# The last expert of a weight load split unevenly over the transfer engines, in an attention and mixture-of-experts kernel

## The chip, the core and the metric

The kernel runs on one core of a Trainium2 chip. A core has a matrix engine (PE, and PEld for its weight loads), a vector engine (DVE), a scalar engine (ACT), GpSimd (POOL), SyncE (SP) and sixteen transfer engines that move data between the chip's memory and the core's on-chip memory of 128 partitions. The metric is the device time of one execution in microseconds (us); lower is better.

## The reference

Attention over 8 batches, 8 heads, 576 positions and 64 numbers a head, with a mask that is a plain window of 32 positions for the first four heads and a dilated one (every fourth of the last 128) for the others. The result, 4608 rows of 512, goes through a soft mixture of 8 experts with 4 slots each:

```python
logits = x @ phi
d = softmax over the rows of logits
slot_input = d.T @ x                      # 32 slots, 4 an expert
for e in range(E):
    h = np.maximum(slot_input[e] @ w1[e], 0.0)   # w1[e]: 512 x 1024
    slot_out[e] = h @ w2[e]                      # w2[e]: 1024 x 512
c = softmax over the slots of logits
out = c @ slot_out
```

All inputs and the output are 32-bit floats in the chip's memory. The kernel works in 16 bits; the loads convert on their way.

## The kernel before

The work is staged as a software pipeline over the eight batches, with an order of steps written out by hand (ORDER). Each batch loads q, k and v (`load_raw`, L201), turns them (L231), forms scores, exponentials and masks, multiplies by v, and from the attention rows forms logits and the running sums of the slot inputs. All transfers of weights, inputs and outputs are issued from POOL's queue, and one list of transfers is worked off in the order of issue, each transfer spread over the sixteen engines.

Weights are loaded between the batches' inputs. The list EARLY holds w1 of experts 0 to 4 one by one, w1 of experts 5 to 7 together, and w2 of experts 0 to 2 together; `load_weights` takes the next ones from it, and `load_full` (L207 for w1, L212 for w2) issues each as one transfer of 128 rows an expert:

```python
EARLY = [(1, e, e + 1) for e in range(5)] + [(1, 5, 8), (2, 0, 3)]
```

One row of w2 of an expert is 4096 numbers, 16 KB in memory and 8 KB on the core. When the input tiles come free, a second transfer loads w2 of experts 3 to 5 (`load_full(late, 2, 3, 6)`, L212 too), and `load_half` (L220) loads w2 of experts 6 and 7 by halves of the columns: expert 6 whole in its half, expert 7 in two quarters, first the left half, then the right.

After the attention stage, PE multiplies the slot inputs by w1 (L608), turns the hidden values (L618), and `emit_so` (L641) accumulates the products with w2, experts 0 to 3, then 4, 5, and the left halves of 6 and 7. `gather_so` (L652) and `spread_so` (L657, L658) bring the left half of the slots' outputs into place, `emit_fin` (L664, L673, L677) forms output tiles of 128 rows, and `emit_batch` issues their stores (L686) from POOL. The right halves of experts 6 and 7 are worked in among the first six batches; the remaining rows are stored last (L713).

Of the kernel before, what the change touches and what calls it, by code (L numbers as in the profile page):

```python
# [10 lines left out]
FP16 = mybir.dt.float16  # L11
# [16 lines left out]
N_SLOTS = 32  # L28
# [16 lines left out]
    (("P", 3), ("P", 4), ("L", 0), ("L", 1), ("D", 0)),  # L45
    (("D", 1), ("D", 2), ("D", 3)),
)
ORDER = """
MD0.2 MK2.2 AP4.2 ET.3 VBc.1 S1.1 MK0.1 RP4.2 ED.3 E1.1 AD1.2 EP.3 VC.1 RD1.2 MP4.2
VCc.1 ER.3 MD1.2 AD3.2 VA.1 QT0.0 AP3.2 RD3.2 VAc.1 QT1.0 RP3.2 MD3.2 S2.1 KT1.0  # L50
# [3 lines left out]
"""  # L54
STEPS = [(w.split(".")[0], int(w.split(".")[1])) for w in ORDER.split()]
ON_ACT = ('D3', 'P0', 'P1', 'P3')
# [40 lines left out]
def kernel(  # L97
# [10 lines left out]
    nc = tc.nc  # L108
# [5 lines left out]
    consts = ctx.enter_context(tc.tile_pool(name="consts", bufs=1))  # L114
# [3 lines left out]
    ident = cst[:, o : o + 128]  # L118
    spread = cst[:, o + 128 : o + 256]
    quad = cst[:, o + 256 : o + 260]  # L120
    masks = consts.tile([128, NMASK], FP16, name="masks")
    phi_raw = consts.tile([128, 4, N_SLOTS], FP16, name="phi_raw")
    phi4 = consts.tile([128, 4, 4, N_SLOTS], FP16, name="phi4")
# [14 lines left out]
    def weights_tile(pool, which, e0, e1):  # L138
        n = (4 * FDIM, 8 * DMODEL)[which - 1]
        t = pool.tile([128, e1 - e0, n], FP16, name=f"w{which}_{e0}", tag=f"w{which}_{e0}")  # L140
        for e in range(e0, e1):
            of = t[:, e - e0]
            if which == 1:
                w1t[e] = of.rearrange("p (c f) -> p c f", c=4)
            else:
                w2t[e] = of.rearrange("p (c n) -> p c n", c=8)
        return t

    EARLY = [(1, e, e + 1) for e in range(5)] + [(1, 5, 8), (2, 0, 3)]
    early_tiles = {x: weights_tile((w1_pool, w2a_pool)[x[0] - 1], *x) for x in EARLY}  # L150
# [54 lines left out]
    def load_full(t, which, e0, e1):  # L205
        if which == 1:
            nc.gpsimd.dma_start(  # L207
                out=t.rearrange("p e (u x) -> p (e u) x", u=2),
                in_=moe_w1[e0:e1].rearrange("e (u p c) f -> p (e u) (c f)", u=2, p=128),
            )  # L210
        else:
            nc.gpsimd.dma_start(  # L212
                out=t, in_=moe_w2[e0:e1].rearrange("e (p c) n -> p e (c n)", p=128)
            )

    def load_half(e, s, n):
        src = moe_w2[e].rearrange("(p c) n -> p c n", p=128)
        cols = slice(DH * s, DH * s + DH)
        for u in range(0, 8, n):
            nc.gpsimd.dma_start(out=w2t[e][:, u : u + n, cols], in_=src[:, u : u + n, cols])  # L220
# [249 lines left out]
    for which in "QK":  # L470
        load_raw(which, 1)
    nc.gpsimd.dma_start(
        out=phi_raw.rearrange("p (u c) s -> p u (c s)", u=2),
        in_=moe_phi.rearrange("(u p c) s -> p u (c s)", u=2, c=2),
# [8 lines left out]
    def load_weights(n):  # L483
        for _ in range(n):
            x = weights.pop(0)
            load_full(early_tiles[x], *x)

    tmp = {}

# [37 lines left out]
    def loads(which, b):  # L527
        load_raw(which, b)
        if which == "V":
            if b > 2:  # L530
                load_weights(1)
            if b == B - 1:
                load_weights(len(weights))
# [6 lines left out]
    for it in range(B + max(s for _, s in STEPS)):  # L540
        for op, stage in STEPS:
            b = it - stage
            if not 0 <= b < B:
                continue
            step(op, b)
            if op in frees and b + 2 < B:
                loads(frees[op], b + 2)
            left.discard((op, b))
            if w2b_pool is None and not left:
                raw_pool.release()  # L550
                w2b_pool = tc.alloc_tile_pool(name="w2b", bufs=1, side="right")
                late = weights_tile(w2b_pool, 2, 3, 6)
                slab_weights(6, "qk0", QK_SLAB)
                slab_weights(7, "qk1", QK_SLAB)
                load_full(late, 2, 3, 6)
                for s in range(2):
                    for e in (6, 7):
                        load_half(e, s, 8 if e == 6 else 4)
        if it == 0:
            nc.vector.tensor_copy(  # L560
                out=phi4, in_=phi_raw[:, :, None, :].broadcast_to([128, 4, 4, N_SLOTS])
            )
# [40 lines left out]
    for fc in range(2):  # L603
        for g in range(2):
            for dc in range(4):
                for j in range(4):
                    e = 4 * g + j
# [9 lines left out]
    for c in range(8):  # L617
# [3 lines left out]
        out=hTm[:, 0].rearrange("p c (j s) -> p c j s", j=4)[:, :, :, 0:16], in_=hT4[:, :, :, 0:16]  # L621
    )
    nc.scalar.copy(
        out=hTm[:, 1].rearrange("p c (j s) -> p c j s", j=4)[:, :, :, 16:32], in_=hT4[:, :, :, 16:32]
# [87 lines left out]
    for e in range(2):  # L712
        nc.gpsimd.dma_start(  # L713
            out=rest[:, e, 512:576, :].rearrange("n i d -> i n d"), in_=om_l[64 * e : 64 * e + 64]
# [37 lines left out]
```

## Time and profile before

| what | before |
|---|---|
| median of 3 runs (lowest to highest) | 178.29 us (178.06 to 178.37) |
| the profiled execution, its own time | 178.29 us |
| its span, first to last instruction | 176.5 us |
| busy: PE, DVE, ACT, POOL | 123.5, 126.0, 123.5, 38.4 us |
| moved by the transfer engines | 40.83 MB counted on the core's side, 231 GB/s |
| read from and written to memory | 62.07 MB and 9.44 MB, 405 GB/s over the span |
| second three-expert load (L212) issued | 105.57 us |
| first output store (L686) issued | 149.40 us |
| last output store (L713) issued | 166.97 us |

Busy times are shares of a span in which stages differ: until some 125 us the batches' pipeline runs on PE, DVE and ACT, then the experts' weights are awaited and used, and from 149 us outputs are stored. The row of the transfer engines counts packets; loads that convert from 32 to 16 bits show half of what they read. The chain of waits is followed back from the last instruction, so it shows which wait set the end and not which engine was busiest.

### The profile page before, as it was taken

The numbers are of one execution on the slowest core, as the hardware profiler recorded it, in microseconds if no ns is written. First come the engines' busy times: TensorE is split into PE (matmuls) and PEld (weight loads), VectorE is DVE, ScalarE is ACT, GpSimd is POOL, SyncE is SP. The second block draws the span as 40 slices with busy tenths as digits, with TensorE's granted clock in tenths as the row PEclk, the third lists the DMA queues.
The fourth block names the chain that finished last, engine by engine and source line by source line (L and its number), as shares of the span: only waits on it lengthen the run. The fifth ranks groups of instructions, "written<-read, shape, count | busy, mean of one in ns | idle before, by whom it ended". The sixth has DMA issues, their size and how long they took to land.

```text
span 176.5 us, 4724 instructions
## 1 busy us (share of the span) xinstructions
PE 123.5 (70%) x2004; PEld 80.9 (46%) x2004; DVE 126.0 (71%) x275; ACT 123.5 (70%) x266; POOL 38.4 (22%) x60
## 2 busy tenths in 40 slices
PE   0026928998888888988989888978677295778300
PEld 0015616676566566656766557656332142221000
DVE  6473899999999999999999998465130104878500
ACT  6007758999999999999999999995501104888300
POOL 7321022112112112116000002710000001856600
PEclk9999999969999999999789999996858969655555
DMA  5999999999999999999999999999999999999997
GB/s 83 215 214 210 214 212 215 215 213 214 216 212 217 211 218 215 208 215 220 213 211 217 213 218 216 222 210 225 213 213 221 192 198 175 340 398 397 401 415 209
DMA packets 18981, 40.83 MB, mean 231 GB/s; under 512 B 1169, under 2 KB 11537, under 8 KB 18193
## 3 DMA queue, kind: packets, MB, share of 16 engines
q0 software_dynamic: 18816, 40.41, 113.8%
q8 instruction: 15, 0.25, 0.5%
q1 hardware_dynamic: 144, 0.14, 0.3%
q14 instruction: 6, 0.04, 0.1%
HBM read 62.07 MB, written 9.44 MB: 405 GB/s over the span
## 4 chain that ended last, share of the span: by engine, by line
ACT 38%; DMA 27%; DVE 14%; PE 10%; issue 2%; POOL 2%; POOLq 0%; ACTq 0%
DMA w<-in_moe_w_dram 19%; ACT p L282 10%; DMA phi_raw<-in_moe_phi_dram 8%; ACT vX L253 7%; ACT xp L337 7%; DVE qk L231 5%; PE f L664 5%; ACT om L673 3%; ACT xT L376 3%; ACT xT L378 3%; DVE p L293 3%; DVE vT L231 3%; ACT xd L337 2%; PE s L273 2%; PE rp L357 2%
## 5 line engine op out<-in xcount | busy, mean ns | idle before, releaser
L282 ACT ACTIVATE p<-s 128x1920 f16<-128x1920 f32 (+1 forms) x24 | 44.6, 1857 | 10.2 <-PE s L273 10.1
L273 PE MATMUL s<-qk 32*128 32x128 f16 (+2 forms) x704 | 26.7, 295 | 18.4 <-DVE qk L231 12.0
L253 ACT COPY vX<-rv 128x768 f16<-128x768 f16 (+1 forms) x32 | 27.8, 943 | 1.8 <-PE rv L247 1.8
L316 PEld LDWEIGHTS <-p 128*128 128x128 f16 (+1 forms) x480 | 22.4, 103 | 13.3 <-DVE xp L341 4.0
L337 ACT ACTIVATE xp<-o_P,rc_P 128x64 f16<-128x64 f32 x96 | 26.5, 497 | 2.2 <-DVE rc_P L328 2.2
L273 PEld LDWEIGHTS <-qk 32*128 32x128 f16 x704 | 17.3, 117 | 21.6 <-DVE qk L231 12.0
L293 DVE TENSOR_TENSOR p<-p,masks 128x1920 f16<-128x1920 f16 (+1 forms) x24 | 25.7, 1084 | 0.2
L231 DVE STREAM_TRANSPOSE qk<-rawQ 128x576 uint32<-128x576 uint32 x16 | 18.8, 1243 | 2.7 <-DMA rawQ<-in_q_dram 2.7
L316 PE MATMUL o_P<-vX,p 128*128 128x65 f16 (+1 forms) x288 | 20.0, 205 | 0.8 <-ACT xp L337 0.2
L231 DVE STREAM_TRANSPOSE qk<-rawK 128x576 uint32<-128x576 uint32 x16 | 19.5, 1231 | 0.4 <-DMA rawK<-in_k_dram 0.4
L247 PE MATMUL rv<-cst,vT 128*128 128x128 f16 x176 | 17.5, 242 | 3.2 <-DVE vT L231 1.8
L231 DVE STREAM_TRANSPOSE vT<-rawV 128x576 uint32<-128x576 uint32 x16 | 19.4, 1223 | 0.5 <-DMA rawV<-in_v_dram 0.5
L686 POOL DMA_DIRECT2D out_dram<-om x15 | 11.1, 744 | 39.2 <-DVE om L677 34.8
L247 PEld LDWEIGHTS <-vT 128*128 128x128 f16 x176 | 13.2, 124 | 7.5 <-issue 3.7
L677 DVE TENSOR_SCALAR om<-f,rrow 128x256 f16<-128x256 f32 (+1 forms) x28 | 13.5, 519 | 3.5 <-PE f L664 2.9
L664 PE MATMUL f<-so_sb,ET 32*128 32x256 f16 (+1 forms) x60 | 12.5, 392 | 3.9 <-ACT om L673 2.7
L673 ACT ACTIVATE om<-f,rrow 128x256 f16<-128x256 f32 (+1 forms) x28 | 12.8, 503 | 2.6 <-PE f L664 2.0
L376 ACT COPY xT<-rp 128x576 f16<-128x576 f16 x16 | 11.5, 909 | 1.3 <-PE rp L357 1.3
L316 PE MATMUL o_D<-vX,p 128*128 128x65 f16 x128 | 9.9, 202 | 2.5 <-DVE xp L341 2.0
L201 POOL DMA_DIRECT2D rawQ<-in_q_dram x8 | 5.1, 633 | 29.4 <-DVE rc_P L328 18.4
L378 ACT COPY xT<-rd 128x576 f16<-128x576 f16 x16 | 10.6, 795 | 0.0
L341 DVE TENSOR_TENSOR xd<-o_D,rc_D 128x256 f16<-128x256 f32 x24 | 9.9, 412 | 0.2
(81 smaller groups left out, 176.7 us busy)
## 6 DMA issues: line engine op xcount, KB each, us to landing
w<-in_moe_w_dram POOLq DMA_DIRECT2D x3, 3072.0 KB, 35.5
out_dram<-om POOLq DMA_DIRECT2D x11, 512.0 KB, 4.6
w<-in_moe_w_dram POOLq DMA_DIRECT2D x5, 1024.0 KB, 15.9
rawQ<-in_q_dram POOLq DMA_DIRECT2D x8, 576.0 KB, 12.7
rawK<-in_k_dram POOLq DMA_DIRECT2D x8, 576.0 KB, 11.4
rawV<-in_v_dram POOLq DMA_DIRECT2D x8, 576.0 KB, 11.6
out_dram<-om POOLq DMA_DIRECT2D x2, 1024.0 KB, 7.3
w<-in_moe_w_dram POOLq DMA_DIRECT2D x2, 512.0 KB, 36.7
```

Source lines behind the costliest of these rows:

```text
L231: nc.vector.transpose(out=out_, in_=in_)
L247: nc.tensor.transpose(rg[:, n_t, :, c, :], rows, ident)
L253: copy(out=vX[b % 2][:, t0 : t0 + n, :, 0:D], in_=rg.rearrange("p n h c d -> p n h (c d)"))
L273: nc.tensor.matmul(sps[:, h, c0 : c0 + w], kk, qq, start=(tt == 0), stop=(tt == 1))
L282: return nc.scalar.activation(out=pt, in_=sps[:, :, 0:n], func=AF.Exp, scale=SCALE)
L293: return nc.vector.tensor_tensor(out=pt, in0=pt, in1=m, op=ALU.mult)
L316: nc.tensor.matmul(o[rows, h, :], lhs, rhs, start=(n == 0), stop=(n == len(jobs) - 1), skip_group_check=True,)
L337: nc.scalar.activation(out=dst[:, h], in_=src[:, h], func=AF.Copy, scale=rc[:, h : h + 1])
L376: copy(out=xT_t[b][:, c, :], in_=rg[:, 0:S])
L378: copy(out=xT_t[b][:, 2 + c, :].rearrange("p (i r) -> p i r", r=DIL), in_=rg[:, :, 0:SUB].rearrange("p r i -> p i r"),)
L664: nc.tensor.matmul(fp[:, 0 : c1 - c0], ET[32 * j : 32 * j + 32, m : m + 128], so_sb[32 * j : 32 * j + 32, c0:c1], start=True, stop=True,)
L673: nc.scalar.activation(out=dst, in_=fp[:, 0 : c1 - c0], func=AF.Copy, scale=rrow[:, blk : blk + 1])
```

## The change

Expert 2 of the early w2 load becomes transfers of its own: 112 rows, then 8, then 8, with three tiny transfers of 13, 8 and 11 rows of 32 numbers (rows of phi, written to a tile that nothing reads) between and behind them. Experts 0 and 1 go as one transfer of the same form as before. The program has six more transfers, all on POOL's queue; every other engine's instructions are the same and in the same order. A transfer whose rows are a multiple of 16 gives each engine the same number of rows. The code takes it that one of fewer rows than 16 uses as many engines as it has rows, starting where the one before it ended, so that 13, 8, 8, 8 and 11 rows, 48 in all, bring that place back to where it was.

```diff
+CURSOR = 13
...
+    aside = consts.tile([16, 3, N_SLOTS], FP16, name="aside")
...
+    def step_cursor(i, n):
+        nc.gpsimd.dma_start(out=aside[0:n, i], in_=moe_phi[0:n])
+
+    def load_uneven(t, e):
+        src = moe_w2[e].rearrange("(p c) n -> p (c n)", p=128)
+        nc.gpsimd.dma_start(out=t[0:112], in_=src[0:112])
+        step_cursor(0, CURSOR)
+        nc.gpsimd.dma_start(out=t[112:120], in_=src[112:120])
+        step_cursor(1, 8)
+        nc.gpsimd.dma_start(out=t[120:128], in_=src[120:128])
+        step_cursor(2, (-CURSOR - 24) % 16)
...
     def load_weights(n):
         for _ in range(n):
             x = weights.pop(0)
-            load_full(early_tiles[x], *x)
+            which, e0, e1 = x
+            if which == 1:
+                load_full(early_tiles[x], 1, e0, e1)
+            else:
+                load_full(early_tiles[x][:, 0 : e1 - e0 - 1], 2, e0, e1 - 1)
+                load_uneven(early_tiles[x][:, e1 - e0 - 1], e1 - 1)
```

## The prediction

> **What bounds the kernel now.** I read the page first: the rows of the DMA and of its queues.
>
> ```profile
> DMA  5999999999999999999999999999999999999997
> GB/s 83 215 214 210 214 212 215 215 213 214 216 212 217 211 218 215 208 215 220 213 211 217 213 218 216 222 210 225 213 213 221 192 198 175 340 398 397 401 415 209
> ...
> q0 software_dynamic: 18816, 40.41, 113.8%
> q8 instruction: 15, 0.25, 0.5%
> ...
> q14 instruction: 6, 0.04, 0.1%
> ```
>
> The sixteen transfer engines are busy from the second slice to the last, so work for them is what the time is made of, and every engine drains its own share in order of issue. The one thing that they don't share evenly is the code: 15 packets of queue q8 bring 0.25 MB, that is 16 KB each, and a packet is one engine's alone. The chain of waits shows where unevenness counts (start, us, what), and the waits name the same pair (us in total, times, longest):
>
> ```profile
> 111.58 0.74 POOL w L220
> 112.33 34.05 DMA w<-in_moe_w_dram
> 146.37 0.04 issue
> 146.41 0.32 PE so L641 x4
> 146.73 0.02 issue
> 146.76 0.43 DVE so_part L652
> ...
> PE so L641 <- DMA w<-in_moe_w_dram: 3.0, 2, 2.3
> ```
>
> At 146.37 the second quarter of expert 7 is complete. It is complete when the slowest of sixteen engines has delivered, and PE, the gather, the spread and the first output store follow at once. Behind it the transfers never run dry: the landings of the output stores follow each other by 1.31 to 1.34 us per 512 KB up to 175.23, about 23.5 us of stores that no engine can shorten. So a shift of the 146.37 us landing shifts the end one for one.
>
> The landing records hold sixteen times for each transfer, one an engine. For the transfer of 146.37 they are: seven engines at 143.71 to 144.47, three at 144.84 to 144.87, six at 145.96 to 146.37. For the first load they all lie within 0.4 us. I sorted the packets into sixteen chains (a packet starts 19 ns before the end of the one ahead of it, so the chains separate). A 16 KB code packet takes 0.89 to 1.07 us and leaves its engine about 1.1 us later for good. Eight engines take the fifteen packets in turn, starting again with the ninth at 86.07. By 146.37 six have been hit twice (the six last ones), two once. The 8 KB packets of q14 add 0.32 us each to three of the other eight. This is the unevenness that the change can touch: give the eight hit engines fewer rows.
>
> **The change part by part.** Before, one transfer brought w2 of experts 0 to 2, 8 rows an engine for each expert. After, experts 0 and 1 go as before; expert 2 goes as 112 rows (7 an engine) and twice 8 rows. If the 13-row transfer leaves the next one to start at engine 13, the two pieces lie on 13, 14, 15, 0 to 4 (the 8-row step goes round to 13 again, the 11-row step back to 0): these eight carry 9 rows of expert 2, engines 5 to 12 carry 7.
>
> *One row.* The 24 rows of the later three-expert transfer take its slowest engine from 126.47 to 141.10: 14.63 / 24 = 0.61 us. So 0.61 us later on the eight heavy engines, 0.61 us sooner on the light ones, and all of it persists, since no engine idles until 149.
>
> *Six more transfers.* On an engine a transfer ends with a 4-byte packet. A 576 KB load repeats every 2.76 us, of which eight packets are 8 x 0.342 = 2.74: 0.02 us for the end. Six times: 0.13. The tiny rows: the phi load has 16 packets of 128 bytes an engine and lands 0.25 us behind the load ahead of it, at most 0.016 us a row; three rows: 0.04. Together 0.16 us on every engine, on the path. From below: 0.1 if the ends hide; from above: 0.3 at 0.05 a transfer.
>
> *Issue.* POOL gets six more issues at some 0.7 us, 4 us in all. They cost nothing, since POOL stands idle there:
>
> ```profile
> 81.33 0.81 POOL L212 DMA_DIRECT2D w<-in_moe_w_dram  x1
> 105.57 0.77 POOL L212 DMA_DIRECT2D w<-in_moe_w_dram  x1 [23.43 <-DVE rc_P L328]
> 106.34 0.90 POOL L220 DMA_DIRECT2D w<-in_moe_w_dram  x1
> ```
>
> The built program has eight completion semaphores in rotation, and an issue waits for the landing of the eighth transfer before it. With six more, the last tiny transfer waits for the fifth w1 load (97.11), the second three-expert load for the 3 MB w1 load (111.91, so it is issued at 112 and not at 105.57), and the six of expert 6 and 7 for landings at 121 to 127. Queued behind them on POOL is only the next load. Engines reach the second three-expert load at 124 to 126 and expert 6 at 138 to 141, so 10 us of cover are left. [...] The first store waits for the last tiny transfer (about 127), not later than now.
>
> *Which engines.* No record names an engine. Records that start in the same nanosecond stand in the file in an order that is no accident: about thirty such pairs whose two chains I can tell apart fit, without one contradiction, a file sorted by engine number as text, with the hit engines being 1 to 8 and hit in the order 4, 5, 6, 7, 8, 1, 2, 3. That is an inference, and it matters more than any price above. If the numbers of the change are the same numbers, light engines 5 to 12 hold only half of the hit ones. Engines 5 to 8 come 0.61 sooner, but 4 and 1, both hit twice by 146.37, get a row more. They stand 2.25 and 2.34 us behind the foremost now (145.96 and 146.05 against 143.71), the last one (engine 6, which started 0.4 us late) 2.66. The new last is 2.34 + 0.61 = 2.95, or 0.29 later than now.
>
> *The sum.* +0.29 (engine 1 is last) + 0.16 (six transfers) = +0.45 us. The profiled execution took 178.29 us (span 176.5, 1.8 around it), which is also the median of the runs shown: 178.74.
>
> *A cost no row shows.* A heavy piece puts 8 rows on 8 neighbouring partitions at once. The nearest row is the store of 64 partitions, sixteen engines on half of the rows: it moves 512 KB in 1.25 us, as the 128-partition store does (2.5 us for 1 MB), so half of the rows cost nothing, and I take 0. From above, a row that takes twice its time costs 0.61 a piece, 1.2 for two, and only where engines arrive together: engines 1 to 3 do. That widens the range upwards; half of it, 0.6, is in the range.
>
> [...]
>
> **The rivals.** *Aligned: faster.* The count that the change turns may stand elsewhere than at 0 when the program starts, or number engines differently, so that the light eight are exactly the hit eight. Then the six late ones land 0.61 sooner (146.37 to 145.76), the others at most 144.87 + 0.61 = 145.48, so the gate moves by -0.61 + 0.16 = -0.45 us: 177.84. For it: the spread is two groups of eight and the change shifts eight against eight by one row, the right size. Against it: my numbering. It decides as soon as no twice-hit engine is heavy.
>
> *No turning: slower.* An 8-row transfer may always begin with engine 0. Both pieces then lie on 0 to 7, five of the six twice-hit engines get a row more, engine 6 among them: +0.61 + 0.16 = +0.77, 179.06. The change would not do what it says. The trace of before has no transfer under 64 rows and can't speak to it. [...]
>
> *Another offset.* The heavy eight lie anywhere else: at least one twice-hit engine is heavy for all but one offset in sixteen, so +0.2 to +0.77.
>
> **How the numbers follow.** Half overlap 0.36, aligned 0.30, no turning 0.20, another offset 0.14. A difference under 0.2% (0.36 us) can't be told from none. Of the half overlap (0.45 with some 0.15 either way) about 0.10 falls under it, of the aligned case (0.45) 0.02, of other offsets 0.02: same 0.14. Faster 0.28, slower 0.58. The range must hold the aligned case with its low overhead and the slow cases with part of the neighbouring-row cost: 177.7 to 179.4. The likeliest case's own range is 178.55 to 179.3.
>
> **What would show it.** The sixteen landings of the second quarter of expert 7: likeliest, the last at about 146.8; aligned, all sixteen within 1.5 us and the last at 145.9; no turning, at 147.1. Landings of the two 8-row pieces wider apart than a row show neighbouring rows in each other's way. POOL's issues must end before 131, and the loads' row must stay at 9 through 110 to 126; a gap there, or a first store not 3.0 us behind the gate, makes the sum wrong. So does another count of code packets than 15.

## The result, and the profile after

| what | before | after |
|---|---|---|
| median of 11 runs each, taken side by side (lowest to highest) | 178.29 us (177.97 to 178.74) | 178.70 us (178.50 to 179.05) |
| ratio, with its 95% interval | 1 | 1.0021 [1.0011, 1.0031] |
| the profiled execution: time, span | 178.29, 176.5 us | 179.05, 177.3 us |
| second quarter of expert 7 complete | 146.37 us | 147.32 us |
| last quarter of expert 7 complete | 151.70 us | 152.22 us |
| first output store issued | 149.40 us | 150.36 us |
| last output store complete | 175.23 us | 175.98 us |

The change costs 0.41 us, 0.2%: slower, and just enough to be told from no change. The profiled execution of after is one of its slowest; it lies 0.35 us above its own median, so the two profiles differ by 0.76 us where the medians differ by 0.41.

The page of after, rows of the transfer engines and of their queues:

```profile
DMA  4999999999999999999999999999999999999997
GB/s 87 211 215 208 216 214 215 213 214 214 219 208 218 211 217 213 216 211 215 217 210 215 214 217 216 224 211 218 213 218 213 194 198 165 307 399 395 401 413 220
...
q0 software_dynamic: 18976, 40.41, 113.4%
q8 instruction: 15, 0.25, 0.5%
...
q14 instruction: 5, 0.04, 0.1%
```

The engines are as full as before, with the same bytes and the same fifteen code packets. The 160 further packets of q0 are those of the six further transfers, of 4 and 64 bytes. So no time was lost to a gap; what is left is how the work is dealt to the engines, and what the further packets take. The chain of waits of after (start, us, what), and behind it the line of its waits (us in total, times, longest):

```profile
127.25 20.07 DMA w<-in_moe_w_dram
147.32 0.04 issue
147.37 0.32 PE so L660 x4
147.68 0.02 issue
147.71 0.44 DVE so_part L671
```

```profile
PE so L660 <- DMA w<-in_moe_w_dram: 3.3, 1, 3.3
```

The same pair as before: PE waits for the second quarter of expert 7 (its last landing is called the gate from here on), 0.95 us later than it did, and gather, spread and first store follow at the same distance (150.36 is 3.04 us behind 147.32; 149.40 was 3.03 behind 146.37). Its sixteen landings, from the records of the transfers, one an engine:

```
before  143.71 143.90 143.91 143.96 143.97 144.25 144.47 | 144.84 144.85 144.87 | 145.96 146.05 146.08 146.09 146.16 146.37
after   143.23 143.43 144.43 144.53 144.62 144.64 144.92 | 145.37 145.45 145.48 145.51 145.59 145.60 145.78 | 146.88 147.32
```

The group of six late engines is gone. Most of it now lies among the seven at 145.4 to 145.8, and two engines stand alone at the end. POOL's timeline (start, us, what; in brackets the idle time ahead of it and what ended that) shows the issues:

```profile
81.80 0.64 POOL L223 DMA_DIRECT2D w<-in_moe_w_dram  x1
83.06 0.55 POOL L219 DMA_DIRECT2D aside<-in_moe_phi_dram  x1 [0.62 <-DMA w<-in_moe_w_dram]
...
97.22 0.50 POOL L219 DMA_DIRECT2D aside<-in_moe_phi_dram  x1 [4.41 <-DMA w<-in_moe_w_dram]
112.30 0.81 POOL L214 DMA_DIRECT2D w<-in_moe_w_dram  x1 [14.58 <-DMA w<-in_moe_w_dram]
121.91 0.94 POOL L234 DMA_DIRECT2D w<-in_moe_w_dram  x1 [8.80 <-PE o_L L330]
126.50 3.87 POOL L234 DMA_DIRECT2D w<-in_moe_w_dram  x5 [3.65 <-PE ep L434]
```

They move as forecast: the last tiny transfer at 97, the second three-expert load at 112 instead of 105.57, the last issue over at 130.4, all ahead of the engines.

### The profile page after: what moved, and what is told of

It is laid out like the page before. It is cut to its first block, busy times and chain, and to the rows that moved or that the text cites. A ratio compares the mean times of both kernels' runs of the same rounds, so it can differ in the third digit from the quotient of the medians.

```text
span 177.3 us, 4730 instructions
## 1 busy us (share of the span) xinstructions
PE 123.3 (70%) x2004; PEld 79.6 (45%) x2004; DVE 125.9 (71%) x275; ACT 123.2 (69%) x266; POOL 41.2 (23%) x66
## 4 chain that ended last, share of the span: by engine, by line
ACT 52%; DMA 19%; PE 11%; DVE 7%; issue 3%; POOL 2%; POOLq 0%; ACTq 0%
ACT p L296 13%; DMA w<-in_moe_w_dram 11%; ACT vX L267 10%; ACT xp L351 9%; DMA phi_raw<-in_moe_phi_dram 8%; ACT xT L390 6%; ACT xT L392 5%; PE f L683 5%; ACT om L692 3%; ACT xd L351 3%; DVE qk L245 2%; DVE vT L245 1%; DVE p L307 1%; ACT ET L426 1%; PE o_P L330 1%
## 5 line engine op out<-in xcount | busy, mean ns | idle before, releaser
L660 PE MATMUL so<-w,hTm 128*32 128x512 f16 (+1 forms) x80 | 7.7, 524 | 3.9 <-DMA w<-in_moe_w_dram 3.3
```

## The experiments

Engines are numbered here by the order in which a short transfer deals its rows: engine 0 gets the first row. In the expectations, theory A says that every short transfer begins at engine 0; theory B of the first four is the one of the change, that a short transfer begins where the one before it ended. The first four and the next four were each timed beside 29 runs of the kernel before (medians 178.35 and 178.30).

### Without the tiny transfers

```diff
         nc.gpsimd.dma_start(out=t[0:112], in_=src[0:112])
-        step_cursor(0, CURSOR)
         nc.gpsimd.dma_start(out=t[112:120], in_=src[112:120])
-        step_cursor(1, 8)
         nc.gpsimd.dma_start(out=t[120:128], in_=src[120:128])
-        step_cursor(2, (-CURSOR - 24) % 16)
```

> Expert 2 as 112, 8 and 8 rows without the three tiny transfers. Theory A (a short transfer always begins at engine 0, so both pieces lie on engines 0 to 7 whatever is between them): the time stays that of the changed kernel less three ends of transfers and their rows, some 0.1 us: 178.6, ratio 1.0015 to 1.002, and the trace shows eight chains with two rows more than the other eight. Theory B (a short transfer begins where the last one ended): the two pieces lie on 0 to 7 and 8 to 15, every engine has 8 rows, and the time is that of before plus two ends, 178.3 to 178.4, ratio about 1.0003.

Measured: 178.53 us, ratio 1.0009 [1.0000, 1.0017]. The records of the packets show both 8-row pieces on the same eight engines. At the landing one engine stands alone, at 146.74, the next at 145.84. The chain of waits ends in it:

```profile
111.95 34.79 DMA w<-in_moe_w_dram
146.74 0.04 issue
```

So the gate is 0.37 us later than before without any tiny transfer, and the median 0.18 us higher, though the interval just reaches 1. It is not the tiny transfers that decide where the pieces lie. Why one engine here and two in after is taken up in the last experiment.

### Another value of CURSOR

```diff
-CURSOR = 13
+CURSOR = 9
```

> CURSOR 9 in place of 13 (tiny transfers of 9, 8 and 15 rows). Theory A: nothing turns, the same eight engines are heavy, ratio 1.002 as with 13. Theory B: the heavy eight are 9 to 15 and 0, the light ones 1 to 8; with the hit engines at 1 to 8, as the prediction inferred, the second quarter of expert 7 lands 0.45 us sooner and the ratio is 0.9975.

Measured: 178.68 us, ratio 1.0016 [1.0004, 1.0027]; two engines alone at the end, 146.83 and 147.15, the next at 145.78.

```profile
127.38 19.77 DMA w<-in_moe_w_dram
147.15 0.04 issue
```

That is the changed kernel over again. With 9 in place of 13 the pieces should have moved by four engines; nothing moved. Nothing turns.

### An even split, with the tiny transfers

```diff
-        nc.gpsimd.dma_start(out=t[112:120], in_=src[112:120])
         step_cursor(1, 8)
-        nc.gpsimd.dma_start(out=t[120:128], in_=src[120:128])
+        nc.gpsimd.dma_start(out=t[112:128], in_=src[112:128])
```

> Expert 2 as 112 and 16 rows (16 rows are one an engine), with the tiny transfers of 13, 8 and 11 rows: five transfers more than before and no unevenness. Both theories: the whole cost is the ends of five transfers and the tiny rows, 0.14 us: 178.43, ratio 1.0008. If the extra transfers or their later issue were the whole loss of the changed kernel, the ratio is 1.002 here too.

Measured: 178.33 us, ratio 1.0001 [0.9991, 1.0011]; the six late engines are back, at 146.00 to 146.13. The interval can't rule out 0.14 us, but the packets give the price. Counted along an engine's packets, the five further transfers take 0.07 us on an engine without a tiny row and 0.13 us on one with all three. The landings agree: their mean over the sixteen engines is 0.08 us ahead of the kernel before at the w1 load in front of the change (110.21 against 110.29) and 0.02 us behind it at the first quarter of expert 7 (143.66 against 143.64). So the further transfers cost some 0.1 us, and the rest of what the change loses, the larger part, comes with its uneven rows.

### Marks behind the loads of the kernel before

Tiny transfers of n rows as marks: 7, 9, 11, 13 and 15 rows behind the w1 loads, and 2, 3, 4, 5, 6 and 8 rows behind the early w2 load, which stays whole. Nothing else differs from the kernel before.

```diff
+    def mark(n):
+        nc.gpsimd.dma_start(out=aside[0:n, n], in_=moe_phi[0:n])
...
+                mark({3: 7, 4: 9, 5: 11, 6: 13, 7: 15}[b])
...
+                for n in (2, 3, 4, 5, 6, 8):
+                    mark(n)
```

> The kernel before with tiny transfers of 7, 9, 11, 13 and 15 rows behind five of the batches' loads and of 2, 3, 4, 5, 6 and 8 rows behind the early w2 load, to tell the engines apart: one with a row of a transfer of n rows takes a 64-byte packet there, one without takes two 4-byte ones. Theory A: the marks are nested (an engine with a row of n has a row of every larger transfer), so each engine's place can be read, with two of the hit eight among 0 to 7 and six among 8 to 15. Theory B: the marks turn, 7 rows on 0 to 6, the next 9 on 7 to 15, and so on, not nested. Time: eleven ends of transfers and rows, some 0.3 us over before.

Measured, one run: 178.59 us. An engine with a row of a mark has a 64-byte packet in its chain; one without has two 4-byte packets instead. The 28 packets of 64 bytes behind the w2 load (2 + 3 + 4 + 5 + 6 + 8) lie nested: an engine that has a row of the 3-row mark has one of all the longer ones. So every short transfer begins at engine 0, and the marks that an engine has give it its number (0 and 1, 9 and 10, 11 and 12, 13 and 14 have the same marks and can't be told apart). The code packets then fall on **engines 5, 6 and 9 to 14**; 0 to 4, 7, 8 and 15 get none, and the q14 packets fall on three of the engines 0 to 3. With this the loss reads plainly: the change gives a row more to engines 0 to 7 and a row less to 8 to 15. Six of the eight engines with code packets gain by it; 5 and 6 get a row on top and are the two at the end.

### Sparing engines 5 and 6

```diff
-        nc.gpsimd.dma_start(out=t[0:112], in_=src[0:112])
-        step_cursor(0, CURSOR)
-        nc.gpsimd.dma_start(out=t[112:120], in_=src[112:120])
-        step_cursor(1, 8)
-        nc.gpsimd.dma_start(out=t[120:128], in_=src[120:128])
-        step_cursor(2, (-CURSOR - 24) % 16)
+        p = 0
+        for n in (112, 8, 5, 3):
+            nc.gpsimd.dma_start(out=t[p : p + n], in_=src[p : p + n])
+            p += n
```

> Expert 2 as 112 + 8 + 5 + 3 rows, no tiny transfers. Theory A (every short transfer begins at engine 0; the engines that carry the code packets are 5, 6 and 9 to 14; the loss came from 5 and 6 having a row more): engines 0 to 2 now carry nine rows, 3 and 4 eight, 5 to 7 seven as the 8-row piece alone gives them back what the 112 rows left out (eight in all, like before), 8 to 15 seven. So 5 and 6 stand as before the change, 9 to 14 a row (0.61 us) sooner, and the last landing of the second quarter of expert 7 is set by 5 or 6 or by an uncoded engine with a row more: 146.1 to 146.4 us, the time -0.1 to -0.3 us against the kernel before, ratio 0.9985 to 0.9996. Theory B (any piece of few neighbouring partitions costs, whichever engines carry it): two short pieces more than an even split cost as the two 8-row pieces did, ratio 1.0009 or above, the last landing 146.7.

Measured: 178.10 us (178.01 to 178.46), ratio 0.9990 [0.9981, 0.9999]. Engines 0 to 2 carry two rows more than in an even split, 3 and 4 one more, 5 to 7 as many, 8 to 15 one less (on engines 0 to 4 that is a row more than the expectation counts). One engine lands at 146.51, the next ten at 145.5 to 146.0:

```profile
121.73 24.78 DMA w<-in_moe_w_dram
146.51 0.04 issue
```

In this profiled execution (178.23, in the upper part of its runs) the gate is no earlier than the 146.37 of before, but the last quarter is complete at 151.51 instead of 151.70, and the last store at 175.16 instead of 175.23. The ratio over eleven runs says more than this pair: 0.2 us faster than before and, by the two ratios, 0.55 us faster than the change, with three short pieces where the change has two. Theory B's price for short pieces is out as the cause of the loss, and this version is the fastest of the three, if by little: its interval against before ends just under 1.

### Twice as many pieces

The loop of the last diff, with other numbers:

```diff
-        for n in (112, 8, 5, 3):
+        for n in (96, 8, 8, 8, 8):
```

> Expert 2 as 96 rows and four times 8 rows, no tiny transfers. Theory A: engines 0 to 7, with 5 and 6 among them, carry two rows more than before the change instead of one, so the last landing of the second quarter of expert 7 and the end come another 0.61 us later than with 112 + 8 + 8: the landing at 147.3, ratio 1.0043 (178.53 + 0.61 = 179.14 against 178.35). Rival (the loss is not in the rows of 5 and 6; it comes from the tail of late landings that varies from run to run): ratio 1.0009 as with 112 + 8 + 8, up to 1.002. If the short transfers turned over the engines, the four pieces would lie on both halves and even out: 1.000.

Measured (six runs): 179.65 us, ratio 1.0076 [1.0063, 1.0088]. Two engines are alone at the end, at 147.34 and 147.47: 1.10 us behind the last one of before, for two rows of 0.61. The direction and the place are theory A's, the size is above its 1.0043. The packets name a part of the rest: between 124 and 126 us many 8 KB packets took 0.7 to 1.1 us where others take 0.625, together 0.20 us an engine. The same is seen with 8 + 5 + 3 (0.22) and faintly with 5 + 5 + 4 + 2 (0.08), and hardly with two pieces (0.02 without the tiny transfers, less with them). What makes it is open; it was not tried alone.

### Half rows of w1 instead

The kernel before with w2 whole; of the w1 load of experts 5 to 7 the last 128 rows, half as long as w2's, are dealt unevenly.

```diff
+            nc.gpsimd.dma_start(out=dst[:, 0:5], in_=src[:, 0:5])
+            p = 0
+            for n in (112, 5, 5, 4, 2):
+                nc.gpsimd.dma_start(out=dst[p : p + n, 5], in_=src[p : p + n, 5])
+                p += n
```

> The kernel before with w2 loaded evenly; instead the last 128 rows of 8 KB in memory of the w1 load of experts 5 to 7 go as 112 + 5 + 5 + 4 + 2 rows. Half the row size of w2's rows, so 0.30 us a row. Theory A: engines 5 to 15, all engines with code packets among them, carry one such row less (-0.30), engines 0 and 1 three more, 2 and 3 two more, 4 one more; four more transfers cost 0.02 to 0.1 us. The last landing of the second quarter of expert 7 at 146.1, the time -0.2 us, ratio 0.9986 to 0.9994. Theory B (pieces of few neighbouring partitions cost by themselves): ratio 1.0005 or above.

Measured: 178.19 us, ratio 0.9994 [0.9985, 1.0003], the last landing at 146.07. Both are where theory A has them, but the interval reaches over 1: as a gain it is not shown.

### Five rows wide

The loop over pieces of w2 once more:

```diff
-        for n in (112, 8, 5, 3):
+        for n in (112, 5, 5, 4, 2):
```

> Expert 2 as 112 + 5 + 5 + 4 + 2 rows, no tiny transfers. Theory A: engines 5 to 15 carry a row less (0.61 us sooner), so all engines with code packets are sooner and the last landing is set by engines 0 and 1 (three rows more, 1.83 us on top of at most 0.8) or 3 (two rows more, 1.22 on top of 1.1): 2.3 to 2.6 us behind the foremost of before, against 2.66 of the engine that was last: -0.1 to -0.3 us at the landing, ratio 0.998 to 1.0005. The sixteen landings then show three or four engines at the end and twelve well ahead. Theory B (pieces of few neighbouring partitions cost by themselves): four short pieces, ratio 1.002 or above.

Measured: 178.33 us, ratio 1.0000 [0.9991, 1.0008]; the last landing 146.47, and ten engines, not four, within 1 us of it. All engines with code packets are spared a row and nothing is gained; engines 0 to 4 carry what the others lost. It looks as if a whole row of 0.61 us is too coarse for what is left, but which engine lands last here is not known.

### Four kernels, profiled a second time

The fifteen code packets took, in order (ns):

```
before           935 974 974 1074 893 893 948 945 | 935 974 975 961 1011 893 948
after            944 935 974 1093 961 892 893 948 | 945 935 974 974 961 893 892
without tinies   948 945 935 1081 974 962 893 893 | 948 944 935 974 975 961 893
```

They repeat with a period of eight, and the three executions begin at the third, the second and the first place of one cycle: 948, 945, 935, 974, 974, 961, 893, 893. In the marked kernel, which begins at the second place, the thirteen packets ahead of 126 us leave the last two and the first of the cycle with one packet, and the engines with one packet are 5, 6 and 9 or 10. So the two of 893 ns are engines 5 and 6. In the execution without tiny transfers only one of them has its second packet ahead of the landing (at 144.32); in after both have (128.58 and 145.25). If the place at which an execution begins is not fixed, this difference is not the work of the tiny transfers.

> A second look at the kernel before, unchanged. The durations of the 15 code packets repeat with a period of eight (948, 945, 935, 974, 974, 961, 893, 893 ns), and the first look began at the third of them (935). If a duration belongs to an engine, and the place in the ring of eight engines at which an execution begins is not fixed (theory P), this look begins at another place in the cycle, 1 chance in 2 at least; which engine is the single or double late one at the second quarter of expert 7 moves with it, the time stays in 178.0 to 178.8. If the place belongs to the program (theory Q), the first packet is 935 ns again.

> A second look at the changed kernel, unchanged. The first look began at the second place of the cycle (945 ns), and the two packets of 893 ns (engines 5 and 6, which carry a row more) came at 128.58 and 145.25: two late landings, 146.88 and 147.32. Theory P (the place belongs to the execution): another place; if it is the first (948), only one 893 ns packet has its second turn before the landing and only one engine stands alone at the end, 146.7 to 146.9; if the third (935), both are late by a row, 146.9 to 147.0. Theory Q (the place belongs to the program): 945 again and two late landings as before, last at 146.9 to 147.3.

> A second look at 112 + 8 + 8 without the tiny transfers. The first look began at the first place (948 ns) and had one late landing, 146.74, the next at 145.84. Theory P: another place, and with the second or third two late landings at 146.8 to 147.2 and a time of 178.6 to 179.0, like the changed kernel's. Theory Q: 948 again, one late landing at 146.7, time 178.46 to 178.66 as in the eleven runs.

> A second look at 96 rows and four times 8. The first look began at the third place (935 ns): both 893 ns packets had their second turn before the landing, two late landings, 147.34 and 147.47, time 179.36, the lowest but one of six runs (median 179.65). Theory P: another place; the time 179.3 to 180.0. Theory Q: 935 again.

Measured, one run each: before begins at 945 this time, after at 945, without tiny transfers at 945, 96 rows and four times 8 at 935 (times 178.56, 178.86, 178.76, 179.51 us). Two of four moved, so the program alone does not set the place. What does is not settled: the second profiles of the last two kernels were taken on another chip than the first ones, and the eleven runs without tiny transfers lie within 0.20 us of each other (178.46 to 178.66), as if there the place had not changed from one to the next. The kernel without tiny transfers, begun at the place of after, now lands like after: two engines alone, at 146.60 and 147.03, and its time (178.76) is that of after. The chains of waits of the four, in the order of the table above and then 96 rows and four times 8:

```profile
114.79 31.84 DMA w<-in_moe_w_dram
146.62 0.04 issue
```

```profile
127.36 19.73 DMA w<-in_moe_w_dram
147.09 0.04 issue
```

```profile
112.27 34.76 DMA w<-in_moe_w_dram
147.03 0.04 issue
```

```profile
126.20 21.19 DMA w<-in_moe_w_dram
147.40 0.04 issue
```

The first shows one thing more: the kernel before, with its gate at 146.62 instead of 146.37. Five of its late engines stand at 146.02 to 146.14 as before, and one at 146.62. Followed along its packets, this engine was the last already at 17 us, 0.36 us behind the next one. The last engine of the first profile was the last there too, by 0.15 us, and it is another one (it has the code packets of 42.73 and 100.74, the other those of 57.43 and 119.75). Behind them the next engines stand at 146.16 and 146.14.

## Why the prediction came out as it did

The time came out as forecast, 178.70 for 178.74, but by a case that the forecast gave a chance of 0.20 and a price of 179.06: no turning. The last landing at 147.1 that it named as the sign of this case came (147.32, and 147.09 in the second profile). The working was right in part and wrong at its most important step, and that the time agrees is luck.

- *What bounds the kernel: right.* The second quarter of expert 7 gates the end, its slowest engine sets it, and code packets make it slow. Undoing the uneven split (1.0001) and doubling it (1.0076) both show in this landing.
- *A shift of the gate shifts the end one for one: right over a few rows, not for the last tenths.* Over the profiles the last store ends 23.5 to 23.9 us behind the last quarter, and 28.6 to 29.1 behind the gate. In after the gate moved by 0.95 and the end by 0.75. Of the 147.32 some 0.4 us is a delay in passing: the code packet of 145.25 lay on that engine, and by the next transfers the last engine is 2.2 us further on (149.53) instead of 2.65.
- *One row, 0.61 us: right.* The packets repeat every 606 ns.
- *Six more transfers, 0.16 us: right where it counts.* In after, the packets give 0.15 us on an engine with all the short rows, as 5 and 6 are, and 0.08 us on one with none.
- *Issue at nothing: right*, with the times of each issue as worked out.
- *Which engines: wrong, twice over.* The transfers do not turn, so the pieces lie on 0 to 7 and not on 13 to 4; and the code packets fall on 5, 6 and 9 to 14 and not on 1 to 8. The numbering came from the order of records that start in the same nanosecond; no contradiction in thirty pairs was not proof, and eight engines in a row was the wrong reading of it. The marks settle this in one run, and no trace of before could have.
- *The term +0.29: right in size by accident.* It stands for two of the six twice-hit engines with a row more and the latest engine of before without one. So it was, but with other engines and by another way: the forecast had 1 and 4 there because of the turning, and it is 5 and 6 because nothing turns. The rival that did happen was priced at +0.77 because, by the wrong numbers, five twice-hit engines would get a row and the latest of before would be among them. In truth that one, last by its late start, is one of 9 to 14. The gate goes from it (146.37, and 146.62 in the second profile) to engine 5 or 6 with a row more (146.7 to 147.3), which is 0.1 to 0.95 us by execution; the medians of the times differ by 0.41.
- *Neighbouring rows at no cost: right for two pieces*, where 0.02 us an engine and less is seen and nothing like 0.61 us a piece; the 0.08 to 0.22 us an engine that came with three and four pieces was not foreseen, and its cause is open.

The turning that the code rests on, no run shows. Every short transfer run here, of 2 to 15 rows and of 8 rows too, begins at the same first engine, and all sixteen take part, those without a row with two 4-byte packets: of the 160 further packets of after, 32 of 64 bytes are the tiny rows, and 128 of 4 bytes are one on each engine for each of the six further transfers and one more on each engine without a row.

## What to carry to other kernels

Where sixteen engines drain shares of one list, as here, the slowest engine sets when a transfer is complete (146.37 us in before, the foremost at 143.71), so look at the sixteen landings of the transfer that gates the end and not at its mean rate. Before an uneven split is designed, mark the engines: a few transfers of 2 to 15 tiny rows show in one run where short transfers begin and which engines carry other traffic. Take rows from those alone (here 0.999 of the time before, hardly more than the noise), and expect the gain to end at the size of a row (0.61 us here) and at what varies from one execution to the next (a gate of 146.37 and of 146.62 in before).

## What the runs showed of the hardware

- A code packet of 16 KB takes one engine 0.89 to 1.09 us and puts its share of a full queue back by about 1.1 us: in the first profile of before the first of the six engines hit twice lands at 145.96, 2.25 us behind the foremost (143.71). Eight of sixteen engines (5, 6, 9 to 14) take these packets in turn, and the place at which the turn begins was not the same in two executions of one program (before: 935 ns first, then 945 ns). For the transfers these packets are a cost here, where their engines are full throughout.
- A transfer of few rows takes an engine without a row 0.01 us (two 4-byte packets, about 6 ns apart) and an engine with a tiny row 0.03 us: a further transfer is nearly free for the engines, and costs POOL 0.50 to 0.64 us of issue.
- The sixteen engines do not start evenly: over the fourteen profiles their first landings lie 0.2 to 0.55 us apart. In both profiles of the unchanged kernel the last starter, not the same engine, stays behind to the end of the loads and sets the gate, 146.37 and 146.62, where the next engine lands at 146.16 and 146.14.
